# The same steps of a chunk-attention and two-layer kernel in another written order

## The chip, the cores and the metric

The kernel runs on one core of a Trainium2 chip. The metric is the device time of one execution in microseconds (us); lower is better. Before the change, three runs took 275.24, 275.53 and 278.67 us; their median is 275.53 us. The profile below is of one execution of its own.

## The reference

Attention inside chunks of 64 tokens, for 8 batches, 8 heads, 576 tokens and a head size of 64, and then two dense layers with a leaky ReLU between them on all 4608 tokens:

```python
q_c = q.reshape(B, H, nc, chunk, D)          # chunk = 64, nc = 9; k and v alike
scores = scale * np.matmul(q_c, k_c.transpose(0, 1, 2, 4, 3))
scores = scores - np.max(scores, axis=-1, keepdims=True)
attn = np.exp(scores)
attn = attn / (np.sum(attn, axis=-1, keepdims=True) + 1e-09)
out = np.matmul(attn, v_c)
x = out.transpose(0, 2, 1, 3).reshape(B * S, H * D)      # 4608 x 512
h = x @ w_in                                             # 512 x 2048
g = np.maximum(0.01 * h, h)
return g @ w_out                                         # 2048 x 512
```

Inputs and output are float32 in HBM.

## The kernel before, in words

**Groups.** The 4608 tokens are cut into 36 groups of 128 (two chunks each). Group `u` goes through a row of small stages, each a step of its own: loads of its q and k rows (`arrive`, 0 for q and 1 for k, issued on POOL, which also converts them to fp16; a group that crosses a batch has two DMAs for each), transposes of q and k, the scores (`s`, PE, eight small matmuls into `Sp`), their maximum and the subtraction (`m`, `b`, DVE), the exponential (`x`, ACT), sum and reciprocal (`z`, DVE), the normalisation (`n`, POOL or DVE, tile `en`), a transpose of the weights, the product with v (`v`, PE, into `xp`) and its copy into `xT` (`a`, ACT). For groups 0 to 9 q and k are transposed on PE (`pe_t`) and copied out (`p` into `QZ`, `k` into `KT`); from group 10 on SP issues transposing DMAs for both (`t`, into `QT` and `KT`) and POOL copies q on into `QZ` (`p`). The weights are transposed on PE for groups 0 to 7 and groups 8, 9 and 18 (`e`, copied by `d2`), else by a transposing DMA on SP (`d`, into `et`).

**Start.** q and k of group 0 come in float32 by DMAs of SP and ACT (L149) and are cast. The v rows of batch 0 are loaded in five pieces (`v_t`, L127) and placed chunk by chunk into the block-diagonal buffer `VB` (`v_p`, ACT, DVE or POOL); the other quarters of both `VB` buffers and of `QZ` are filled with zeros (`zv`, `zq`). v of a later batch comes in two DMAs (`v_in`, L111). `w_in` comes in four blocks of 512 columns, each in two halves (`Q`, L135), and `w_out` in four blocks of 512 rows (`P`, L141).

**Layers.** The tokens form 12 blocks: four of 128 and eight of 512. Blocks 0 to 3 are plain: 16 matmuls of 128 columns for each quarter of the first layer (`mm1`, L187, into `hT`), leaky ReLU on ACT (`g`, into `gT`), the second layer in quarters (`mm2`, L212, into `oP`). Block 4 and 5 have the plain first layer in pieces of 256 tokens. From block 6 on the first layer, and from block 4 on the second, use a seven-product scheme (Strassen's, in Winograd's form): sums of inputs (`xf`, tile `XF`, L285), of hidden values (`sf`, tiles `S` and `gT`) and of weights (`vf`, `wf`, tiles `VF` and `WF`), products (`f`, L325, into `hA`, `hB`, `hC`; `m2`, L373, into `oA`, `oB`, `oC`), and additions of the results on DVE and ACT. Stores go out from SP (`save`).

**The order of the work.** Every step is created once, by `add`, with an engine and a function that emits its instructions. Nothing is planned at run time: `ORDER` is a written list of 1403 entries, and `run` emits step after step from it:

```python
for i, fill, *slots in ORDER:
    s = steps[i]
    if fill:
        idle(fill[0], BANKS[fill[1]])
```

Each engine executes its own instructions in this order, and each instruction waits for what it needs. So the place of a step in the list sets what stands ahead of it on its engine; a step that waits holds up all behind it on that engine, DMA issues on POOL and SP included. The slots name the PSUM bank or the temporary tile. `fill` puts matmuls on constants ahead of a PE step (`idle`, L538; so many units of 128 columns); they are executed whether PE would have to wait or not. `ON` says which engine takes a step that can run on several.

## Time and profile before

| | us |
|---|---|
| median of three runs | 275.53 |
| profiled execution, its span | 275.67 |
| PE, busy | 263.9 |
| DVE, busy | 209.4 |
| ACT, busy | 196.3 |
| POOL, busy | 158.2 |

The page gives a span of 275.7 us and nothing around it. PE, DVE, ACT, POOL and SP are TensorE's matmuls, VectorE, ScalarE, GpSimd and SyncE; PEld is TensorE's weight load, which overlaps the matmuls. Engines run side by side, so their shares don't add up. L187 is line 187 of the kernel. In a timeline a row has start, duration, engine, line and operation, output and input, count and, in brackets, how long the engine idled before and what ended that. A DMA is issued by an engine and lands later; the time from issue to landing has its own view. The last matmul ends at 272.2 us; an eviction on ACT of 0.38 us and a store follow.

### The profile page before, as it was taken

The page shows a single profiled execution, that of the slowest core. Times are in us where ns is not written, and L with a number is a line of the kernel's source. Part 1 is how long each engine was busy: PE and PEld are TensorE (multiplying, and loading weights), DVE is VectorE, ACT ScalarE, POOL GpSimd, SP SyncE. Part 2 cuts the span into 40 slices and gives each one's busy share as a digit, 9 for nine tenths or more (in the row PEclk, how much of TensorE's full clock was granted, in tenths as well). Part 3 has the DMA queues.
Part 4 walks back from the last instruction along what each step waited for, and adds up shares of the span by engine and source line. Part 5 has one row for each costly group of instructions (what it writes and reads, how often), then busy time and mean ns, then how long its engine had stood idle before and what let it go on. Part 6 is the DMA issues. An engine that isn't in the chain of part 4 may idle for free.

```text
span 275.7 us, 7655 instructions
## 1 busy us (share of the span) xinstructions
PE 263.9 (96%) x3099; PEld 230.8 (84%) x3099; DVE 209.4 (76%) x376; ACT 196.3 (71%) x370; POOL 158.2 (57%) x199
## 2 busy tenths in 40 slices
PE   4899999999999999999799999999999999999994
PEld 2459678788898899999799999999999989888884
DVE  5786276878889898799778997889998873825462
ACT  6478964767844834899698558899787897467821
POOL 8989685595999991928927888626752020000000
PEclk9999999999999999999999999999999999999999
DMA  9999999999999999999999999969972051040016
GB/s 133 158 190 179 179 167 175 134 157 168 172 160 148 173 173 183 132 138 223 129 131 198 138 173 199 153 148 131 212 154 40 0 137 58 0 155 0 30 49 231
DMA packets 163635, 38.64 MB, mean 140 GB/s; under 512 B 154640, under 2 KB 159248, under 8 KB 163600
## 3 DMA queue, kind: packets, MB, share of 16 engines
q0 software_dynamic: 114384, 18.09, 101.9%
q1 hardware_dynamic: 48176, 19.80, 40.1%
q8 instruction: 24, 0.39, 0.6%
q10 hardware_dynamic: 1040, 0.26, 0.4%
q14 instruction: 11, 0.09, 0.1%
HBM read 36.70 MB, written 9.44 MB: 167 GB/s over the span
## 4 chain that ended last, share of the span: by engine, by line
PE 87%; DMA 5%; ACT 5%; POOL 1%; issue 1%; POOLq 0%
PE oA L373 20%; PE hA L325 14%; PE hT L187 13%; PE oC L373 10%; PE hC L325 7%; PE oB L373 5%; PE oP L212 5%; PE hB L325 4%; PE Sp L453 3%; DMA KT<-k_in 3%; PE xp L519 3%; DMA k_in<-in_k_dram 2%; PE idle L538 1%; ACT VB L118 1%; ACT xT L532 1%; ACT gT L198 1%
## 5 line engine op out<-in xcount | busy, mean ns | idle before, releaser
L373 PEld LDWEIGHTS <-gT 128*128 128x128 f16 x640 | 61.3, 98 | 6.7
L489 POOL TENSOR_TENSOR en<-ex,zi 128x512 f16<-128x512 f16 x23 | 26.5, 1153 | 48.4 <-DVE zi L483 17.3
L237 DVE TENSOR_TENSOR tmp<-hC,tmp 128x512 f32<-128x512 f32 x48 | 32.1, 683 | 20.0 <-PE hC L325 18.3
L187 PE MATMUL hT<-xT,w_inT 128*128 128x128 f16 (+1 forms) x512 | 46.0, 246 | 1.0 <-ACT xT L532 0.9
L187 PEld LDWEIGHTS <-w_inT 128*128 128x128 f16 x512 | 39.4, 98 | 4.7 <-issue 1.3
L325 PEld LDWEIGHTS <-VF 128*128 128x128 f16 x512 | 39.4, 98 | 2.7
L93 POOL DMA_DIRECT2D q_in<-in_q_dram x39 | 33.6, 866 | 5.2 <-DMA w_outT<-in_moe_w_out_dram 2.1
L93 POOL DMA_DIRECT2D k_in<-in_k_dram x39 | 33.6, 865 | 2.3 <-DMA k_in<-in_k_dram 1.2
L446 POOL COPY QZ<-QT 64x512 f16<-64x512 f16 x52 | 33.2, 639 | 2.7 <-DMA QT<-q_in 0.5
L201 ACT ACTIVATE tmp<-hA 128x512 f32<-128x512 f32 x48 | 27.7, 598 | 8.6 <-PE hA L325 8.0
L198 ACT ACTIVATE gT<-hT 128x512 f16<-128x512 f32 x48 | 26.7, 601 | 8.6 <-PE hT L187 8.6
L373 PE MATMUL oA<-WF,gT 128*128 128x256 f16 x256 | 32.5, 273 | 0.0
L325 PEld LDWEIGHTS <-w_inT 128*128 128x128 f16 x384 | 30.2, 98 | 2.3
L463 DVE TENSOR_REDUCE mx<-Sp 128x8 f32<-128x512 f32 x36 | 24.5, 682 | 8.6 <-PE Sp L453 8.5
L198 ACT ACTIVATE gT<-tmp 128x512 f16<-128x512 f32 x48 | 29.6, 629 | 1.2 <-DVE tmp L237 1.2
L473 ACT ACTIVATE ex<-sh 128x512 f16<-128x512 f32 x36 | 22.7, 629 | 10.3 <-DVE sh L467 10.1
L479 DVE TENSOR_REDUCE z<-ex 128x8 f32<-128x512 f16 x36 | 24.3, 676 | 6.2 <-ACT ex L473 6.1
L325 PE MATMUL hA<-XF,VF 128*128 128x128 f16 (+1 forms) x256 | 27.5, 246 | 0.0
L532 ACT ACTIVATE xT<-xp 128x512 f16<-128x512 f32 x36 | 21.2, 599 | 8.7 <-PE xp L519 8.6
L373 PEld LDWEIGHTS <-S 128*128 128x128 f16 x256 | 24.5, 98 | 2.7
L467 DVE TENSOR_TENSOR sh<-Sp,mx 128x512 f32<-128x512 f32 x36 | 24.4, 683 | 0.5
L201 ACT ACTIVATE hB<-hA 128x512 f32<-128x512 f32 x24 | 13.9, 586 | 12.2 <-PE hA L325 12.1
(77 smaller groups left out, 490.3 us busy)
## 6 DMA issues: line engine op xcount, KB each, us to landing
out_dram<-osb SPq DMA_DIRECT2D x14, 512.0 KB, 4.3
VB<-in_v_dram POOLq DMA_DIRECT2D x14, 288.0 KB, 7.8
q_in<-in_q_dram POOLq DMA_DIRECT2D x31, 128.0 KB, 7.4
k_in<-in_k_dram POOLq DMA_DIRECT2D x31, 128.0 KB, 7.2
w_inT<-in_moe_w_in_dram POOLq DMA_DIRECT2D x8, 256.0 KB, 7.6
w_outT<-in_moe_w_out_dram POOLq DMA_DIRECT2D x4, 512.0 KB, 9.4
out_dram<-osb SPq DMA_DIRECT2D x6, 256.0 KB, 4.9
v_t<-in_v_dram POOLq DMA_DIRECT2D x4, 128.0 KB, 7.6
```

The source lines that it names most:

```text
L93: nc.gpsimd.dma_start(out=t[a - u * G:z - u * G], in_=src[b, :, r:r + z - a, :].rearrange("h p d -> p h d"))
L187: nc.tensor.matmul(out=hT[:, i, :], lhsT=w_inT[:, t, fc * 128:(fc + 1) * 128], rhs=xT[:, t, r0 % RING:r0 % RING + tb], start=(i == 0 and t ...
L198: nc.scalar.activation(out=to, in_=of, func=AFT.Prelu, bias=0.0, scale=1.0, alpha=0.01)
L201: nc.scalar.activation(out=to, in_=of, func=AFT.Copy, bias=0.0, scale=1.0)
L237: (nc.vector if e == "dve" else nc.gpsimd).tensor_tensor(out=to, in0=a, in1=b, op=ALU.add)
L325: nc.tensor.matmul(out=PA[key][:, c, :], lhsT=w[:, t, fc * 128:(fc + 1) * 128], rhs=x[:, t, :], start=(m in (1, 5) and c == 0 and t == 0), ...
L373: nc.tensor.matmul(out=to, lhsT=lhs[:, fc, p * 128:(p + 1) * 128], rhs=rhs[:, fc, :], start=(fresh and fc == 0), stop=(fc == HB - 1), skip ...
L446: nc.gpsimd.tensor_copy(out=QZ[u % NQZ][part, :, :, s, :], in_=QT[u][part].rearrange("p i (e t) -> p i e t", e=2))
L463: nc.vector.tensor_reduce(out=MX[u], in_=SP[u], axis=AXL.X, op=ALU.max)
L467: nc.vector.tensor_tensor(out=SH[u], in0=SP.pop(u), in1=MX.pop(u).unsqueeze(2).to_broadcast((128, 8, CH)), op=ALU.subtract)
L479: nc.vector.tensor_reduce(out=z, in_=E[u], axis=AXL.X, op=ALU.add)
L489: eng.tensor_tensor(out=E[u], in0=ex, in1=ZI.pop(u).unsqueeze(2).to_broadcast((128, 8, CH)), op=ALU.mult)
```

## The change

The steps are the same 1403, with the same shapes. `ORDER` and `ON` are written anew, and the code around them is shortened.

**The order in the front.** By names (for `arrive`, q1 is group 1's q rows), POOL had:

```
q1 k1 k2 Q0 Q0 identity q2 q3 v0 v1 v2 k3 Q1 zq3 Q1 Q2 Q2 q5 v3 v_p v_p v_p q4 P0 zv k5 P1 zv zv zv
k4 q6 k7 v4 P2 k6 v_p q7 Q3 Q3 v_in1 v_in1 P3 q8 ...
```

and has now:

```
identity q3 q2 k1 k2 q1 k5 k3 v1 v0 v2 Q1 Q2 Q2 Q1 Q0 Q0 q4 v_p v_p v3 q5 v_p v_p k4 P0 n3 v_p Q3 Q3
v_p P1 P2 k7 q7 k6 v4 q6 v_in1 v_in1 P3 v_p n4 k8 ...
```

PE had, up to the first pieces of the layers (fillers in brackets, in units of 128 columns):

```
[21] k0 q0 q1 k1 [3] s0 k2 s1 [47] q3 q2 e0 [13] s2 [9] e1 [9] v0 k3 [6] v1 mm1(0,0) mm1(1,0) s3 mm1(0,1) e2
mm1(1,1) v2 mm1(0,2) mm1(1,2) mm1(2,0) q4 ...
```

and has now (`mm1(j,a)` is block j, quarter a of `w_in`):

```
[32] q0 [2] k0 [14] s0 q2 q3 [19] k1 [9] k2 [9] q1 [23] s2 [4] s1 k3 e0 k5 [25] s3 [44] v0 [6] e1 [13] v1
[2] mm1(0,1) e2 mm1(1,2) v2 mm1(0,2) mm1(2,1) mm1(0,0) mm1(2,0) q4 q5 e3 mm1(1,1) mm1(2,2) k4 v3 mm1(1,0)
mm1(3,1) mm2(0,0) mm1(3,2) s4 mm2(2,0) s5 mm1(3,3) ...
```

All fillers together were 108 units and are 202. ACT now has, from the first placed v row to the second xT: `v_p zv d2(0) k3 v_p v_p x1 v_p v_p v_p v_p x2 d2(1) a0 a1`, then `g a2 x3`.

**The order later.** DVE now has, around group 10: `m10 wf1 b10 n9 sf(4,0) d2(9) sf(4,1) z10 m11 b11 m12 z11 b12 m13 n11 b13`; it had `m10 b9 b10 z8 z9 vf0 z10 n10 sf(4,0) sf(4,1) sf(4,3) m11 b11`. PE has, around group 9: `v9 m2(4,5) s11 mm1(5,6)`; it had `v9` directly before block 5's `mm1`. SP had `save(4,1) t22q t23q d19 save(5,0) t22k d20` and has `t22q save(4,1) t22k t23q t24q d19 save(5,0) t23k d20`; near group 33 it had `t33q save(7,1) t33k t34k t34q d30 save(7,0)` and has `t33q t34q save(7,0) t35q t33k d30 t34k`.

**The engines.** 191 steps are on POOL instead of 186, 296 on DVE instead of 301; PE, ACT and SP keep their number. Seven of the 32 `xf` sums move from DVE to POOL: two of block 6, one of block 7, two of block 8, one each of blocks 10 and 11. As many `n` steps as before, 23, are on POOL, but others: `n3`, `n4` and `n7` come to it. Four `zv` fills and one `zq` fill leave POOL, and of the 18 `v_p` copies it has seven instead of four.

**The code.** Tiles that rotated through one tag with several buffers get a tag for each buffer, chosen by the group's or block's number; the windows of two q tiles become single tiles; branches that were never taken go (loads of pairs of q rows among them). Some steps name more of what they wait for, which matters to whoever plans an order and not to the instructions:

```diff
-    def k_tile():
-        return sbp.tile([128, H, D], FP16, name="k_in", tag="k_in", bufs=NIN)
+    def in_tile(what, u):
+        return sbp.tile([128, H, D], FP16, name=what, tag=f"{what}{u % NIN}", bufs=1)
...
+    IN_Q: dict[int, bass.AP] = {}
+    IN_K: dict[int, bass.AP] = {}
...
     def load_q(u):
-        load_rows(q_tile(u), q, u)
-        qk[u] = (q_tile(u), qk[u][1] if u in qk else None)
+        IN_Q[u] = in_tile("q_in", u)
+        load_rows(IN_Q[u], q, u)
...
-    def x_form(j, h, i):
+    def x_form(j, h, i, e):
...
         def less(to, a, b):
-            (nc.gpsimd if j >= POOL_X else nc.vector).tensor_tensor(out=to, in0=a, in1=b, op=ALU.subtract)
+            minus(to, a, b, e)
...
-        E[u] = sbp.tile([128, 8, CH], FP16, name="en", tag="en", bufs=3)
+        E[u] = sbp.tile([128, 8, CH], FP16, name="en", tag=f"en{u % 3}", bufs=1)
...
     ORDER = [
-        (55, 0), (0, 0), (56, 0), (62, 0), (1, 0), (59, 0), (60, 0), (64, 0), (61, 0), (2, 0), (57, 0), (63, 0), (65, 0), (3, 0), (66, 0), (4, 0), (52, 0), (5, 0),
...
+        (5, 0), (61, 0), (55, 0), (7, 0), (58, 0), (6, 0), (57, 0), (63, 0), (66, 0), (1, 0), (2, 0), (52, 0), (83, (32, 7), 0), (0, 0), (54, 0), (53, 0),
...
-        p1 = mm(1, 0, xs + gone(j) + [get(("fast", x)) for x in fast_n[-LIMIT:-LIMIT + 1]], [A], spare=SPARE + 1)
+        p1 = mm(1, 0, xs + gone(j) + w11 + [get(("fast", x)) for x in fast_n[-LIMIT:-LIMIT + 1]], [A], spare=SPARE + 1)
...
-                out_.append(add(key + (name, p), "act", us[0], emit, [of[p]] if last else of, key=7.0 + k0 / 100, take=T[name] if p == 0 else []))
+                out_.append(add(key + (name, p), "act", us[0], emit, [of[p]] + out_ if last else of, key=7.0 + k0 / 100, take=T[name] if p == 0 else []))
...
-                add(("xf", j, h, i), "pool" if j >= POOL_X else "dve", 1.6 if j >= POOL_X else dve, lambda j=j, h=h, i=i: x_form(j, h, i),
+                e, us = on(("xf", j, h, i), "dve", dve=0.40 if wide == 512 else 0.34, pool=1.6)
+                add(("xf", j, h, i), e, us, lambda j=j, h=h, i=i, e=e: x_form(j, h, i, e),
```

## The prediction

> **What bounds the kernel now.** I read the page first: the span, the busy shares and the slices.

> ```profile
> span 275.7 us, 7655 instructions
> PE 263.9 (96%) x3099; PEld 230.8 (84%) x3099; DVE 209.4 (76%) x376; ACT 196.3 (71%) x370; POOL 158.2 (57%) x199
> PE   4899999999999999999799999999999999999994
> DMA  9999999999999999999999999969972051040016
> ```

> PE is full in every slice but the first two, one near the middle and the last. DMA is full for 26 slices too, so transfers can still hold PE up. To see how much room is left I summed PE by stretches (after the stretch: its length, then the busy time of PE, PEld, DVE, ACT and POOL, the granted clock, DMA and GB/s) and listed what PE waited for after 20 us (total, times, longest).

> ```profile
> 0.00:20.00 20.00, 14.69 (x112) 8.29 (x113) 14.22 (x34) 12.06 (x23) 17.55 (x29) 1.00 1.51 160
> 20.00:272.20 252.20, 249.21 (x2993) 222.55 (x2989) 195.18 (x343) 183.91 (x347) 140.61 (x171) 1.00 1.44 139
> 272.20:275.70 3.50, 0.02 (x1) 0.00 (x0) 0.00 (x0) 0.38 (x1) 0.00 (x0) 1.00 0.38 135
> ```
> ```profile
> PE Sp L453 <- DMA KT<-k_in: 1.7, 1, 1.7
> PE hT L187 <- ACT xT L532: 0.9, 2, 0.7
> PE tpe L497 <- ACT gT L198: 0.3, 1, 0.3
> ```

> So the time is a sum of four terms: the start of the first layer's matmuls (20.0, below); PE's work from there (249.2); the waits in it (252.2 - 249.2 = 3.0, of which the three rows name 2.9); and 3.5 of last eviction and store. The granted clock is 1.00 in every stretch. Because every step is kept, with its shapes, the 249.2 can't be reordered away. The change can move only the start and the waits.

> The start, from the timelines of PE, POOL and ACT (start, duration):

> ```profile
> 1.46 2.42 PE L538 MATMUL idle<-XF 128*128 128x512 f16 x6 [1.46 <-DVE zeros L157]
> 5.94 0.58 PE L411 MATMUL kp<-ident,k_in 128*128 128x128 f16 x4 [2.06 <-POOL ident masks.py:199]
> 9.92 0.61 PE L411 MATMUL kp<-ident,k_in 128*128 128x128 f16 x4 [1.05 <-DMA k_in<-in_k_dram]
> 10.76 4.16 PE L538 MATMUL idle<-XF 128*128 128x512 f16 x12
> 18.75 0.39 PE L519 MATMUL xp<-et,VB 128*128 128x64 f16 x8
> 18.98 0.39 PE L411 MATMUL kp<-ident,k_in 128*128 128x128 f16 x4
> 19.98 2.17 PE L187 MATMUL hT<-xT,w_inT 128*128 128x128 f16 x32
> ```
> ```profile
> 1.24 1.07 POOL L93 DMA_DIRECT2D q_in<-in_q_dram  x1 [0.79 <-POOLq L1160]
> 5.26 0.27 POOL masks.py:197 MEMSET ident<- 128x128 f16 x1
> 5.60 0.29 POOL masks.py:199 TENSOR_SCALAR_AFFINE_SELECT ident<-ident 128x128 f16<-128x128 f16 x1
> 7.61 2.65 POOL L127 DMA_DIRECT2D v_t<-in_v_dram  x3
> 14.41 0.61 POOL L135 DMA_DIRECT2D w_inT<-in_moe_w_in_dram  x1 [0.15 <-issue]
> ```
> ```profile
> 16.84 2.44 ACT L118 ACTIVATE VB<-v_t 64x256 f16<-64x256 f16 x6
> 19.31 0.60 ACT L532 ACTIVATE xT<-xp 128x512 f16<-128x512 f32 x1
> 19.93 0.63 ACT L473 ACTIVATE ex<-sh 128x512 f16<-128x512 f32 x1
> ```

> The first hT starts when ACT has written xT of the first group (19.31 + 0.60 = 19.9). Ahead of that ACT places v rows for 2.4. The second stretch above begins there, at 20.0.

> Two pieces of the chain of waits (start, duration) give the price of a first-layer piece, 16 matmuls of 128 columns, and of a second-layer piece:

> ```profile
> 30.41 0.86 PE oP L212 x4
> 35.63 0.89 PE hT L187 x16
> ```

> **The front, step by step.** The identity now precedes all loads on POOL: 5.26 to 5.84 was 0.6, so the first load goes out at 1.8 instead of 1.2. Then come ten row loads (q3 q2 k1 k2 q1 k5 k3 v1 v0 v2) where before there were eight with two weight halves among them. The DMA view of short windows gives the issue-to-landing times (count, KB, us) of the first row load, of the third v load and of the last half of the third weight block:

> ```profile
> q_in<-in_q_dram POOLq DMA_DIRECT2D x1, 128.0 KB, 4.9
> ```
> ```profile
> v_t<-in_v_dram POOLq DMA_DIRECT2D x1, 128.0 KB, 7.5
> ```
> ```profile
> w_inT<-in_moe_w_in_dram POOLq DMA_DIRECT2D x1, 256.0 KB, 8.3
> ```

> POOL needs 0.88 per row load (2.65 / 3). Before, v2 was issued at 9.4 and landed at 16.9, and the last half of block 2 at 14.4 + 8.3 = 22.7. Between them lie one row and four halves, 5.8 in all; with 0.6 for the row a half takes 1.3. After, v2 is the tenth load: issued at 1.8 + 9 x 0.88 = 9.7, landing between 14.6 (4.9 later) and 17.2 (7.5 later). I take the middle, 15.9, because the queue is filling then. The first matmuls now want w_in block 1, whose second half is the fourth behind v2: 15.9 + 4 x 1.3 = 21.1. Block 0, which had lain ready early, lands last, at 15.9 + 7.8 = 23.7; its first user stands four matmul pieces later (21 + 4 x 0.89 + 0.5 = 25), so that is covered by 1.3.

> ACT gives nearly the same start. v1 lands two loads ahead of v2, at 14.2. Then ACT's written order to the first xT is seven v copies (2.44 / 6 = 0.41 each, 2.9), a zero fill, two copies and an exponential (2.4 by the 0.60 and 0.63 rows): 19.5. Then exponential, copy and xT, 1.8: 21.3. PE's own queue gives it a third time. It holds 202 filler units, against 108. The first 32 are slow (2.42 / 21 = 0.115 each): 1.46 + 3.7 = 5.1. The other 170 at 0.055 (0.89 / 16) are 9.4, with 1.0 on top while the clock is still low, and of 17 small stages four take 0.6 and thirteen 0.23 (18.75 to 18.98): 5.4. That is 20.9. So the start is **21.3**, between 20.0 (landing at 14.6) and 22.6 (17.2). Seventeen small PE stages instead of fifteen lie ahead of it, so PE's remaining work falls by 2 x 0.23: 248.75.

> [...]

> **The waits.** The longest, 1.7, is a K transpose that stood on SP behind an output store:

> ```profile
> 124.47 1.20 SPq L508 DMA_TRANSPOSE et<-en  x1
> 126.61 0.38 SPq L385 DMA_DIRECT2D out_dram<-osb  x1
> 127.16 1.96 SPq L433 DMA_TRANSPOSE KT<-k_in  x1
> ```

> This is group 22's; in the new order it stands before that store and before the et transpose at 124.47, so it goes out at least 2.7 earlier and the 1.7 goes. The other two follow v stages:

> ```profile
> 75.71 1.91 PE L187 MATMUL hT<-xT,w_inT 128*128 128x256 f16 x16 [0.69 <-ACT xT L532]
> 89.71 0.49 PE L187 MATMUL hT<-xT,w_inT 128*128 128x256 f16 x3 [0.22 <-ACT xT L532]
> ```

> The 0.69 was group 9, whose xT was wanted straight after its v stage; now a layer-2 piece and a score stage stand between (1.1), so it goes too. The 0.22 of group 11 stays: two score stages and the v stage itself, 0.7, lie ahead of the user in both orders.

> New ones are late next, at about 73 to 92 us. Counted in PE pieces, the score stage of group 10 moves 5 us back and its v stage only 2. DVE's queue between them is now: maximum, a weight difference, subtract, normalise of group 9, a layer-2 sum, a copy, another sum, and group 10's normaliser. Two groups of instructions (busy, mean ns of one, idle before) and a row of the DMA issues price these:

> ```profile
> L237 DVE TENSOR_TENSOR S<-gT 128x2048 f16<-128x2048 f16 x8 | 10.0, 1252 | 1.4 <-ACT gT L198 1.4
> L467 DVE TENSOR_TENSOR sh<-Sp,mx 128x512 f32<-128x512 f32 x36 | 24.4, 683 | 0.5
> L489 POOL TENSOR_TENSOR en<-ex,zi 128x512 f16<-128x512 f16 x23 | 26.5, 1153 | 48.4 <-DVE zi L483 17.3
> ```
> ```profile
> et<-en SPq DMA_TRANSPOSE x25, 5.1
> ```

> The pieces ahead put the score of group 10 at 69.1 and its v stage at 84.1. From 69.4, four steps of 0.7, three of 1.25 and 0.8 of small ones bring DVE to 76.8; POOL's normalise, 1.15, and the transpose, 5.1, to 83.1. One us is left for all hand-overs, and two K transposes stand close behind on SP. I allow 0.3 each for groups 9 and 10, 0.4 for group 11 (its et transpose is behind those two), 0.2 for its xT and 0.2 for a layer-2 sum that ends about one us before its use: **1.4**, between 0.2 (only group 11's xT) and 3.0 (as many as before).

> **Moves between engines.** Seven of the 32 input sums go from DVE to POOL. Their smallest form on DVE is this:

> ```profile
> L285 DVE TENSOR_TENSOR XF<-xT,XF 128x256 f16<-128x256 f16 x8 | 2.6, 328 | 0.0
> ```

> POOL running that form isn't in the trace: at least 0.33 by this row, at most about 2.3 by twice POOL's 1153 ns, which is the nearest row and whose 1.2 I take. Seven times that, 8, fits in the 48.4 that POOL idles before its normalise steps alone. Without that cover each load queued behind one would go out up to 2.3 later. In the front POOL loses five zero fills and gets three v copies more, which I count at nothing: it sits in the gaps between loads.

> Tile names with fixed slots instead of rotating ones reuse the same buffers in the same turn; I cost them at nothing, between -0.3 and +0.3, the size of one such wait.

> **Sum.** 21.3 + 248.75 + 1.4 + 3.5 = 274.95 of span. The median of before stands 0.15 below its profiled span (275.53 to 275.7), so **274.8**. With the bounds above, 20.0 to 22.6 and 0.2 to 3.0, it is 272.3 to 277.7.

> **Rivals.** Nothing ends late (chance 0.15): the start is halfway to the quickest landing, 20.6, and only group 11's wait is left: 20.6 + 248.75 + 0.2 + 3.5 - 0.15 = 272.9. For it: two of three named waits are removed by order alone. Against: three chains (weights, ACT, fillers) all end near 21.

> PE still slow (0.10): fillers are issued whether needed or not. If the clock comes up at 14 as before, the 37 units that fall between 8 and 14 cost 0.06 more each, 2.2, of which I let 0.4 hide behind loads: the start 23.1, the time 276.6. For it is the 0.61 at 9.92; against it, the gaps of 2.06 and 1.05 that kept PE from a steady run are filled now.

> POOL blocked, slower (0.17): the normalise step of group 3 now stands on POOL behind w_out block 0 and ahead of w_in block 3 and w_out blocks 1 and 2; before, DVE did it. That w_out block lands at 23.7 + 4 x 0.6 + 2 x 1.3 = 28.7, so it is issued 7.5 before, and POOL gets to the step at about 22.0. Its input waits for xT of group 2 (21.3, two pieces, two stages and 0.8: 24.4), the exponential and the normaliser, 0.6 + 1.2: 26.2; with 1.15 and a 0.4 copy the next load goes out at 27.8. That is 5.8 without an issue, against 2.6 of queue (7.5 - 4.9). The second half of block 3 then lands at 33.9 to 36.5, and is wanted at 21.3 + 13.6 = 34.9 (eleven pieces of 0.89, two of 0.86 and nine stages of 0.23). It decides from a landing after 34.9; every us later is paid once, and the w_out blocks behind it add theirs: 2 to 5, so 277 to 280, at the middle 278.3.

> Transposes late on SP (0.13): group 33's K transpose now stands behind a store and group 35's Q. If it or two others cost what the 1.7 did, 274.8 + 1.7 to 5.1: 276.5 to 280, middle 278.2.

> **Numbers.** The forecast keeps 0.45. From 272.6 to 279.5 all but the ends of the first rival and of the last two are held, about 2 in 10. A measurement of this kernel can tell about 2% from no change (270.0 and 281.0). Below 270.0 the start and the waits would have to lose 5.5 of 23.0 (20.0 + 3.0) while three chains end near 21: 0.02. Above 281.0: the tails of the last two rivals, 0.08. Within: 0.90.

> **What would show it.** The first hT at 21.3, released by ACT xT or by w_inT; PE busy 248 to 249 after it; no wait on KT at 133; small waits on xp or xT near 75 to 90; 3.5 after the last matmul. Wrong would be a wait on w_inT or w_outT near 35 to 40 (POOL blocked), fillers at over 0.1 a unit after 8 us (slow PE), or a wait of over 1.5 on KT or et.

## The result, and the profile after

The changed kernel takes 286.82 us (median; 283.35 to 289.61 over four executions) against 275.41 us for the kernel before. The ratio is 1.0339, with a 95% interval of 1.0247 to 1.0431: slower by 3.4%. The ratios leave out executions more than 1.5% above the fastest of their kernel, so they can stand below the quotient of two medians, and the profiles of four runs below (the K transposes first, the filled wait, all four repairs, the mended order with room) are of such longer executions, so that what they show holds for these executions.

The profiled execution took 286.58 us and has a span of 284.5. First the page: span, PE's share, and then the 40 slices of PE, of its granted clock and of DMA.

```profile
span 284.5 us, 7720 instructions
PE 270.0 (95%) x3124; PEld 231.9 (82%) x3124; DVE 210.4 (74%) x371; ACT 195.5 (69%) x370; POOL 162.8 (57%) x204
PE   7899998999996899999899899999999999999995
PEclk9999999999999799999999999999999999999999
DMA  9999999999999999999999999999792330101043
```

PE is nearly as full as before (95 and 96%), but not at the same places: there are dips in the 13th, the 20th and the 23rd slice, and the clock has a dip in the 14th (92 to 100 us). The sum by stretches, cut at the first hT and at the last matmul (length, busy time of PE, PEld, DVE, ACT, POOL, clock, DMA, GB/s):

```profile
0.00:21.26 21.26, 18.17 (x148) 9.52 (x149) 17.31 (x40) 16.88 (x31) 18.58 (x31) 1.00 1.53 154
21.26:281.01 259.75, 251.82 (x2976) 222.40 (x2976) 193.05 (x332) 178.28 (x339) 144.26 (x174) 0.99 1.34 134
281.01:284.50 3.49, 0.00 (x0) 0.00 (x0) 0.00 (x0) 0.38 (x1) 0.00 (x0) 1.00 0.36 130
```

So the start is 21.26, PE works 251.82, waits 259.75 - 251.82 = 7.93, and the tail is 3.49. The longest of these waits by what ended them (from 21.26 us on; total, times, longest):

```profile
PE xp L491 <- DMA et<-en: 6.0, 4, 2.8
PE hT L169 <- DVE sh L439: 0.5, 1, 0.5
PE qp L388 <- DMA q_in<-in_q_dram: 0.4, 1, 0.4
```

Six of the eight us are the values stage (`xp`) waiting for the transposed weights (`et`) of a group: 2.79 at group 11, 1.04 at 19, 1.98 at 21, 0.19 at 27. The wait for a K transpose that stood first before the change is gone. PE's timeline around the longest (start, duration; in brackets the idle time before), and the windows on both sides of 94.48:

```profile
93.04 0.41 PE L491 MATMUL xp<-et,VB 128*128 128x64 f16 x8 [2.79 <-DMA et<-en]
94.13 5.32 PE L169 MATMUL hT<-xT,w_inT 128*128 128x256 f16 x32 [0.22 <-ACT xT L504]
100.16 3.66 PE L169 MATMUL hT<-xT,w_inT 128*128 128x256 f16 x32
```
```profile
91.06:94.48 3.42, 1.22 (x28) 1.09 (x29) 3.35 (x5) 0.99 (x3) 2.81 (x4) 1.00 1.82 157
94.48:97.89 3.41, 3.41 (x19) 2.43 (x17) 3.38 (x6) 2.14 (x5) 3.41 (x4) 0.50 3.31 99
```

32 matmuls that take 3.66 us at 100 us took 5.32 at 94, since the clock was at half for 3.41 us. That is 3.41 / 2 = 1.7 us lost behind a wait of 2.79.

### The profile page after: what moved, and what is told of

It reads as the page before. It is cut to its first block, busy times and chain, and to the rows that moved or that the text cites. A ratio compares the mean times of both kernels' runs of the same rounds, so it can differ in the third digit from the quotient of the medians.

```text
span 284.5 us, 7720 instructions
## 1 busy us (share of the span) xinstructions
PE 270.0 (95%) x3124; PEld 231.9 (82%) x3124; DVE 210.4 (74%) x371; ACT 195.5 (69%) x370; POOL 162.8 (57%) x204
## 4 chain that ended last, share of the span: by engine, by line
PE 66%; DMA 13%; DVE 7%; ACT 7%; POOL 4%; issue 2%; POOLq 0%; DVEq 0%; ACTq 0%
PE oA L355 16%; PE hA L307 12%; PE hT L169 9%; PE oC L355 8%; DMA et<-en 8%; PE hC L307 6%; PE oB L355 4%; DMA q_in<-in_q_dram 4%; PE hB L307 3%; PE xp L491 3%; PE Sp L425 2%; DMA k_f<-in_k_dram 2%; POOL k_in L79 1%; PE oP L194 1%; DVE z L451 1%
## 5 line engine op out<-in xcount | busy, mean ns | idle before, releaser
L169 PE MATMUL hT<-xT,w_inT 128*128 128x128 f16 (+1 forms) x512 | 47.5, 250 | 0.8 <-DVE sh L439 0.5
L461 POOL TENSOR_TENSOR en<-ex,zi 128x512 f16<-128x512 f16 x23 | 24.7, 1073 | 32.5 <-DVE zi L455 14.6
L418 POOL COPY QZ<-QT 64x512 f16<-64x512 f16 x52 | 36.0, 696 | 5.6 <-DMA QT<-q_in 3.9
L451 DVE TENSOR_REDUCE z<-ex 128x8 f32<-128x512 f16 x36 | 24.4, 677 | 5.0 <-ACT ex L445 4.9
L445 ACT ACTIVATE ex<-sh 128x512 f16<-128x512 f32 x36 | 22.6, 631 | 6.0 <-DVE sh L439 5.8
L183 ACT ACTIVATE hB<-hA 128x512 f32<-128x512 f32 x24 | 13.7, 583 | 11.1 <-PE hA L307 10.4
## 6 DMA issues: line engine op xcount, KB each, us to landing
q_in<-in_q_dram POOLq DMA_DIRECT2D x31, 128.0 KB, 6.0
k_in<-in_k_dram POOLq DMA_DIRECT2D x31, 128.0 KB, 6.1
w_inT<-in_moe_w_in_dram POOLq DMA_DIRECT2D x8, 256.0 KB, 8.0
out_dram<-osb SPq DMA_DIRECT2D x6, 256.0 KB, 4.2
v_t<-in_v_dram POOLq DMA_DIRECT2D x4, 128.0 KB, 5.6
```

The source lines that it names most:

```text
L169: nc.tensor.matmul(out=hT[:, i, :], lhsT=w_inT[:, t, fc * 128:(fc + 1) * 128], rhs=xT[:, t, r0 % RING:r0 % RING + tb], start=(i == 0 and t ...
L183: nc.scalar.activation(out=to, in_=of, func=AFT.Copy, bias=0.0, scale=1.0)
L418: nc.gpsimd.tensor_copy(out=QZ[u % NQZ][part, :, :, s, :], in_=QT[u][part].rearrange("p i (e t) -> p i e t", e=2))
L451: nc.vector.tensor_reduce(out=z, in_=E[u], axis=AXL.X, op=ALU.add)
L461: eng.tensor_tensor(out=E[u], in0=ex, in1=ZI.pop(u).unsqueeze(2).to_broadcast((128, 8, CH)), op=ALU.mult)
```

## The experiments

**The old order in the new code.** The lists `ORDER` and `ON` of the kernel before, written into the changed kernel.

```diff
-    ON, ORDER of the change
+    ON, ORDER of the kernel before, by step name
```

> The changed kernel's code with the order and the engines of the kernel before written into it (54 steps go back to their old engine; tags and helper functions stay those of the changed kernel). Theory A (the loss lies in the written order alone): 275.4 us, within 0.3% of the kernel before, start at 20.0 us, no wait over 1.8 us. Rival (some of the loss comes with the code around the order, such as the fixed buffer tags): 277 us or more.

Measured: 275.69 us against 275.82, ratio 0.9995 (0.9969 to 1.0020). The profiled execution took 275.27 with a span of 273.5. By the same stretches:

```profile
0.00:19.04 19.04, 13.14 (x111) 7.56 (x112) 14.68 (x36) 12.49 (x23) 17.48 (x29) 1.00 1.55 158
19.04:270.06 251.02, 249.26 (x2994) 222.55 (x2990) 195.64 (x341) 183.61 (x347) 142.33 (x171) 1.00 1.41 140
270.06:273.50 3.44, 0.00 (x0) 0.00 (x0) 0.00 (x0) 0.38 (x1) 0.00 (x0) 0.86 0.37 134
```

The loss is in the two lists alone: within the interval, tags and shortened code cost nothing. Order and engines change together here and in the hybrids below, so what the engines of the 54 steps bear by themselves was not tested. This is also the better base: the execution profiled before the change started its first hT at 19.98 and waited 3.0, this one 19.04 and 1.76. Against it, the change costs 2.22 in the start, 6.17 in waits, 2.56 in PE's work and 0.05 in the tail: 11.0, the difference of the spans (284.5 - 273.5).

**The K transposes first.** SP's list around group 11:

```diff
-    t15q save(0,0) d10 t14k t15k d11 t16q
+    t15q save(0,0) t15k t14k d10 d11 t16q
```

> The changed kernel with SP's K transposes of groups 15 and 14 issued ahead of the et transpose of group 10 instead of behind it (two entries of the order move, nothing else). Theory A (group 11's et transpose is late because SP sat waiting for group 10's normalisation, and its two K transposes then went into the queue just ahead of it): it lands at about 90.3 us instead of 92.99, the wait of 2.79 us at group 11's values falls below 0.8, with it goes the 3.41 us of half clock, worth 1.7; up to 2 us of the gain may be given back at groups 21 and 23, whose et transposes wait for themselves: 282 to 284.5 us. Theory B (the transposes are slow because the two value loads of batch 3, issued at 80.81 and 82.55, share the transfer engines with them): it lands no earlier than 92, the wait stays over 2 us, 286 to 287.

Measured: 289.27 us, ratio 1.0377 (1.0289 to 1.0465). SP's timeline and PE's:

```profile
77.33 6.40 SPq L412 DMA_TRANSPOSE KT<-k_in  x2
83.82 2.67 SPq L480 DMA_TRANSPOSE et<-en  x2
```
```profile
90.78 0.61 PE L491 MATMUL xp<-et,VB 128*128 128x64 f16 x8 [4.72 <-DMA et<-en]
```

The rows for group 14's K transpose landed at 82.5 in this execution, SP stood at it until then, and now group 10's et transpose was late, by 4.72. Group 11's went out at 85.19 and landed at 92.51, which speaks against theory A and for theory B. But two transposes had still gone out just ahead of it, at 82.54 and 83.82, so this run doesn't separate the two; the next one does, since it leaves SP's list as it is.

**The value loads later.** POOL's list:

```diff
-    v_in3 p14 v_in3 k17 k16 p15 p15 q18
+    p14 k17 k16 p15 p15 q18 v_in3 v_in3
```

> The changed kernel with the two value loads of batch 3 issued on POOL behind the next three row loads, about 3 us later (needed first by group 13 at 109.5 us); SP's order stays. Theory B (the transposes are slow because these loads share the transfer engines): group 11's et transpose, issued at 84.9, takes about the median of 5.1 us instead of 8.10, lands near 90, the wait of 2.79 and the half clock behind it go: 282 to 284.5 us. Theory A (the place in SP's queue): it still takes 7 to 8 us, the wait stays over 2 us, 286 to 287.

Measured: 285.83 us, ratio 1.0353 (1.0314 to 1.0392). The DMA view in 0.1 us at the issue of group 11's et transpose, of the changed kernel and then of this one: the queue of POOL's loads and SP's queue (packets, MB, and the time that the packets took, added up, as a share of the time of 16 DMA engines, which can pass 100%), and the transpose's time to landing:

```profile
q0 software_dynamic: 100, 0.01, 199.5%
q1 hardware_dynamic: 5, 0.00, 9.7%
et<-en SPq DMA_TRANSPOSE x1, 8.1
```
```profile
q0 software_dynamic: 19, 0.00, 116.9%
q1 hardware_dynamic: 68, 0.02, 76.5%
et<-en SPq DMA_TRANSPOSE x1, 3.9
```

Theory B holds for this wait, and theory A falls: the K transposes of groups 14 and 15 still went out just ahead, at 81.35 and 82.64, and the transpose took 3.9 instead of 8.1. Over the whole flight of the transpose SP's queue has 56% in the changed kernel and 68% here, POOL's 149% and 106%: the two value loads held the engines while the transposes got less of them. Group 11 didn't wait, and the clock stayed full there. But the time didn't follow: 282 to 284.5 was expected. What was late next was a score bank that DVE frees, and group 21's transpose:

```profile
PE xp L491 <- DMA et<-en: 3.7, 2, 2.9
PE hT L169 <- DVE sh L439: 2.0, 1, 2.0
```

The 2.9 fell in group 21, and there the clock fell to half for 3.41 us.

**Filled wait.** Twelve idle products ahead of group 11's values (they took 2.75 us, from 90.73):

```diff
-    PE: m2(5,1) v11
+    PE: m2(5,1) [48 units] v11
```

> The changed kernel with 12 idle products (48 units of 128 columns, 2.56 us at full clock) ahead of group 11's values, so that TensorE works while it waits for the same transpose; nothing else. Theory C (the half clock of 94.5 to 97.9 us is set off by the idle 2.79 us, and costs about 1.7 us by itself): the clock stays full, the transpose lands at 93.0 as before, the span falls by 1.3 to 1.7 at 100 us, of which up to 1 may be given back at groups 19 and 21: 285 to 285.5 us. Rival (the clock falls for another reason, such as the power of the work behind it): the half clock stays, 286.5 to 287.

Measured: 287.05 us, ratio 1.0367 (1.0313 to 1.0422). The two windows here are the one behind group 11's wait and the one behind group 21's:

```profile
94.82:98.23 3.41, 3.19 (x34) 2.79 (x31) 3.38 (x5) 3.39 (x8) 3.41 (x4) 1.00 3.13 101
159.67:163.08 3.41, 3.41 (x35) 2.91 (x32) 0.06 (x1) 0.00 (x0) 3.32 (x6) 0.50 2.10 172
```

The clock stayed full at 94.8, so theory C holds: with the same work behind it and the idle time filled (0.62 us idle in the window ahead, 2.20 in the changed kernel's), the fall is gone. Group 11's values started 1.07 us later than in the changed kernel (94.11 against 93.04), group 16's scores 0.59 earlier (104.81 against 105.40): 1.66 won, as priced. It was given back at groups 19 and 21: group 21's values waited 3.21 and the clock fell there instead. My expectation of the total was wrong by that.

**Group 21 earlier.** Its normaliser, its normalisation and two transposes move; DVE and SP:

```diff
-    sf(6,1) xf(7) xf(7) xf(7) m22 xf(7) +u3 b22 +u3 sf(6,2) z21
+    sf(6,1) z21 xf(7) xf(7) xf(7) m22 xf(7) +u3 b22 +u3 sf(6,2)
-    d20 t25q t26q save(5,1) t24k d21
+    d20 d21 t25q t24k t26q save(5,1)
```

> The changed kernel with group 21's normaliser moved ahead of four input sums, three output sums, a maximum, a subtraction and a hidden-value sum on DVE (it ended at 148.3 us though its exponential was done at 139.9), its normalisation ahead of a value load on POOL, and on SP its et transpose and the K transpose of group 24 ahead of the Q transposes of groups 25 and 26. Theory A (the end of the run hangs on group 21's values, which come 1.98 us late, and this lateness is made by the written order of DVE, POOL and SP): the et transpose goes out near 142 instead of 151.74 and lands by 152, the wait of 1.98 goes; group 19's 1.04 and the 2.79 of group 11 stay: 283.5 to 285. Rival (the transfers are so full there that whatever is moved forward pushes another transfer late): a wait of 1.5 us or more comes at the next score stage or values stage, 286 to 287.

Measured: 284.82 us, ratio 1.0278 (1.0195 to 1.0361). The timelines of ACT, DVE and SP in the changed kernel show what was there: group 21's exponential, its sum eight us later, and two Q transposes of which the second stood until its rows had landed.

```profile
139.20 0.65 ACT L445 ACTIVATE ex<-sh 128x512 f16<-128x512 f32 x1
147.10 0.67 DVE L451 TENSOR_REDUCE z<-ex 128x8 f32<-128x512 f16 x1
142.01 7.35 SPq L409 DMA_TRANSPOSE QT<-q_in  x2
```

The 1.98 at group 21 went, a smaller wait, 0.85, came at group 23, and group 19's grew from 1.04 to 1.48; in sum PE waited 7.27 instead of 7.93. Theory A held for that one place.

**All four repairs.** That one, the later value loads, the maxima of groups 14 and 15 and the first one's subtraction (`m14 b14 m15`) ahead of a weight sum and a hidden-value sum on DVE, and

```diff
-    t23q t24q d19
+    d19 t23q t24q
```

> The changed kernel with four repairs of its order: the value loads of batch 3 three row loads later (as in the run of that alone), group 14's and 15's maximum and subtraction ahead of two weight and hidden-value sums on DVE (they held a score bank for 1.97 us once the first repair was in), group 19's et transpose ahead of two Q transposes on SP, and group 21's normaliser, normalisation and transposes early. Theory A (the loss behind the start is four or five waits, each made by one place in the order, and one fall of the clock): waits on et in sum below 2 us, the clock full from 6 us on, 277 to 280 us. Rival (the order is late as a whole by 70 us, and each repair uncovers the next wait): 282 to 285.

Measured: 284.13 us, ratio 1.0240 (1.0152 to 1.0328): the rival. PE's waits were still 8.07, at other places, and the clock fell once, behind group 23's wait:

```profile
PE xp L491 <- DMA et<-en: 2.3, 1, 2.3
PE Sp L425 <- POOL QZ L418: 2.3, 2, 1.4
PE oC L355 <- DVE osb L219: 1.5, 1, 1.5
```

**Where in the order.** Four hybrids, cut at an entry of `ORDER`; each step takes the engine that goes with its part.

```diff
-    ORDER = new
+    ORDER = new[:130] + the rest as in old       (and with 280)
+    ORDER = old[:280] + the rest as in new       (and with 130)
```

> The first 130 entries of the new order (to 27.5 us: the run of row loads and the run of weight blocks that the change is named after) with their engines, then all other steps in the old order with the old engines; 11 temporary buffers or banks are renumbered. Theory D (the front by itself costs only what it forecast, 1.3 us of later start less 0.5 of work done earlier, and the loss lies in the order behind it): 276 to 278 us, no wait over 2 us after 30 us. Theory E (the new front leaves rows and weights late, and that makes the waits at 90 to 160 us): 281 us or more.

> The first 280 entries of the new order (to 60.7 us), the rest in the old order; 12 buffers are renumbered. Theory D1 (the loss lies behind entry 280: DVE's, POOL's and SP's order around groups 10 to 21): 276 to 279 us. Theory D2 (by entry 280 the new order has fallen behind with the scores: group 10's stand at 70.75 us instead of 64.0, because its rows were loaded later): waits on et or QZ of 3 us or more in sum between 65 and 100 us, 280 us or more.

> The first 280 entries of the old order (to 59 us), then all other steps in the new order with the new engines; 9 buffers are renumbered. Theory G (the parts of the new order add their losses, and the part behind 60 us has its own: the new front with the old rest cost 6.3 us, so 4 to 5 are left): 279.5 to 282 us, with waits on et of 2 us or more in sum. Theory H (the later part is only late because the new front hands over late): 275 to 277.5 us, waits as in the kernel before.

> The first 130 entries of the old order (to 26 us), then the new order; nothing is renumbered. Theory G: the loss of the first 130 entries, 2.6 us, is gone and the rest stays, 283 to 285 us. Theory H: well below 281.

| kernel | us | ratio (95%) | first hT | PE's waits behind it | half clock |
|---|---|---|---|---|---|
| new to 130, then old | 278.91 | 1.0094 (1.0065 to 1.0122) | 21.87 | 2.64 | none |
| new to 280, then old | 282.57 | 1.0211 (1.0138 to 1.0284) | 21.76 | 4.86 | none |
| old to 280, then new | 285.96 | 1.0292 (1.0226 to 1.0357) | 18.80 | 8.91 | 2 x 3.41 |
| old to 130, then new | 287.26 | 1.0397 (1.0352 to 1.0441) | 18.29 | 9.52 | 1 x 3.41 |
| changed kernel | 286.82 | 1.0339 (1.0247 to 1.0431) | 21.26 | 7.93 | 1 x 3.41 |

The run of row loads and weight blocks costs 2.6 us by itself (1.0094 of 276.3), most of it a later start (21.87 against the control's 19.04): theory D in kind, 0.9 above its range. Theory E and theory H fall: the rest of the new order is slow behind the old front too. But theory G, by which the losses of the parts add, missed as well, by 4.0 and 2.3 us at the upper ends of its two ranges, and the new front to 280 fits neither of its theories: it took more than the 279 of the one, and its longest wait, 2.30, stays below the 3 of the other. The waits of the old front to 280 with the new rest show whose they are:

```profile
PE xp L491 <- DMA et<-en: 4.7, 4, 3.1
PE xp L491 <- DVE et L102: 1.4, 1, 1.4
PE xp L491 <- DVE osb L219: 1.0, 1, 1.0
```

The first and third rows are groups 10, 11, 19 and 21 again. The shares of the parts can't be read more closely than that, because a cut makes waits of its own: the 1.4 stands five us behind the cut, the hybrid with the new front to 280 waits 2.30 at group 7, at 67.5, and the one with the old front to 130 waits 2.05 and 1.30 for two K rows, at 28.8 and 31.9.

**Room instead of repairs.** Between a group's scores and its values on PE lie other pieces. At their own prices (0.87 for most, 0.44 for a product of the first layer, 0.23 for a small stage) they, with the scores themselves, are the room for the chain of DVE, ACT, POOL and SP. Group 11 had 14.3 us of room in the old order and has 12.3 in the new; group 21 had 27.9 and has 18.9. The chains took 15.9 and 22.5 in the changed kernel. Room alone doesn't decide: groups 32 and 33 have 14.0 and 13.6 in the new order and don't wait. One run gives room by moving only PE's stages (and with group 20's its copy on ACT):

```diff
-    m2(6,2) v20 v21 f(7) ... m2(6,4) v22
+    m2(6,2) f(7) ... m2(6,4) v20 v21 v22
```

> The changed kernel with the values stages of groups 20 and 21 moved on PE from behind the product m2(6,7) to just ahead of group 22's, some nine pieces (8 us) later; nothing else, no transfer and no sum moves. Their result is first needed by the input sums of block 8, after group 23's. Theory F (a wait is what PE's order leaves too little room for: without waits 18.9 us of PE work lie between group 21's scores and its values, the chain of DVE, ACT, POOL and the transposing DMA took 22.5): the wait of 1.98 us goes, the others stay, 284 to 285.5. Rival (the order is late as a whole, and what is won shows as the next wait, at group 23's or 24's): the sum of PE's waits stays at 8 us, 286 to 287.

Measured: 284.01 us, ratio 1.0291 (1.0202 to 1.0381). Group 21's wait is gone with nothing in its place; PE's waits are 5.80, and this holds for theory F. What is left on `et` is group 11's 2.96 and group 19's 1.19:

```profile
PE xp L491 <- DMA et<-en: 4.1, 2, 3.0
```

Two more begin the chains of groups 10 and 11 earlier (`p10` ahead of `n8` on POOL, `s10` and `s11` each six pieces of 0.87 earlier on PE, and what follows them), alone and together with all the rest:

> The changed kernel with the chain of groups 10 and 11 begun earlier: their four QZ copies on POOL ahead of or directly behind group 8's normalisation (where POOL idled 3.2 us), their scores on PE four and five pieces earlier, and behind them the maxima, subtractions, exponentials, normalisers, normalisations and et transposes. Theory F (the wait of 2.79 at group 11 and the fall of the clock behind it come from too little room between scores and values: 12.3 us of PE work against a chain of 15.9): the et transposes of groups 10 and 11 land 3 us or more ahead of their use, no wait on et before 130 us, the clock stays full at 93 to 100, PE's waits at 70 to 100 us fall from 5.7 us (clock included) to below 2: 282 to 284.5. Rival (the transfers hold it): group 11's et transpose still lands after 92.

> Both of these together with the repairs of the run before (value loads of batch 3 later, group 14's and 15's maximum and subtraction earlier, group 19's et transpose, group 21's normaliser earlier) and group 23's K transpose ahead of its Q transpose. Theory F (each wait is a chain with too little room, and room given at groups 10, 11, 20 and 21 removes waits without a new one): PE's waits after the start, 12.1 us with the clock in the changed kernel, fall to 4 to 6, and the time to 278 to 281. Rival (each repair uncovers the next wait): 10 us or more of waits are left, 283 to 285.

Measured: 285.54 us (1.0309, 1.0180 to 1.0437) and 285.29 us (1.0301, 1.0221 to 1.0381). In both of these runs groups 10 and 11 don't wait, and the clock stays full. But 7.40 and 6.60 us of waits are left, and both times missed theory F's ranges. In the second no wait for an et DMA stands among the long ones; these do:

```profile
PE hT L169 <- DVE sh L439: 1.8, 1, 1.8
PE oC L355 <- DVE osb L219: 1.5, 1, 1.5
PE hA L307 <- DVE XF L216: 1.3, 1, 1.3
PE xp L491 <- DVE et L102: 1.2, 1, 1.2
```

By the lists, each is made by a step that had been pushed back for one that was moved ahead. The last run mends these four:

> The order with room for groups 10, 11, 20 and 21, its own bad places mended: group 10's scores take a bank that is wanted 4 us later (PE had waited 1.8 us for it), group 9's et copy stands ahead of group 11's normaliser again (1.15), a sum of block 4's output ahead of two others (1.5), group 21's normaliser behind block 7's fourth input sum (1.3). Theory F (single waits, each with its place): these 5.7 us go, PE's waits after the start fall from 8.9 to 3 to 5 us, 279 to 281 us. Rival (each repair uncovers the next wait): 7 us or more are left, 283 or more.

Measured: 285.63 us, ratio 1.0316 (1.0247 to 1.0385). The four are gone, and others stand there:

```profile
PE Sp L425 <- POOL QZ L418: 3.7, 1, 3.7
PE oA L355 <- DVE S L216: 2.4, 2, 1.3
```

POOL had waited 5.74 us for group 24's Q transpose, and group 23's copies stood behind it. SP's list is that of the run before, where this transpose went out even later (136.34 against 135.63) and PE waited for nothing there: it took 3.73 us then and 7.52 here. Here a value load had gone out 0.20 us ahead of it, in the run before 0.39 behind it; whether that is the cause was not tested. The rival holds: repairs at single places moved the waits, and took 2.8 us off the median at the most, which the intervals don't separate from the changed kernel. No order with the new rest came below 284 us in the median, so why the new rest is late as a whole stays open.

## Why the prediction was wrong

The forecast was 274.8 us, the range 272.6 to 279.5. The profiled execution took 286.58, which is 11.8 more. By the sum's own terms: start 0.0 (21.26 for 21.3), PE's work +3.1 (251.82 for 248.75), waits +6.5 (7.93 for 1.4), tail 0.0, time against span +2.2 (2.08 above it for 0.15 below).

**The front: right, but against the wrong base.** The three estimates of the start, 21.1 by the weights, 21.3 by ACT and 20.9 by PE's fillers, met the run: the last half of `w_in` block 1 landed at 21.13, ACT's first xT ended at 21.12 and the last filler at 21.18. Which of the three set the 21.26 can't be told. The identity first, the ten row loads, the fillers and `n3` on POOL did what was worked out; PE waited neither on `w_outT` nor on `w_inT`. POOL blocked, the rival at 278.3, is out. So is PE still slow: the clock was full from 5.73 us on, against 13.73 in the profile before (the record of the clock begins with that rise, so the views print 1.00 ahead of it; eight idle products of 512 columns took 3.60 us there, at 1.46, and eleven took 2.54 behind it, at 16.10). In the twelve profiles with the new front it came up at 4.2 to 6.3 us, in the four with the old one, where PE waits 2 us and more among the first pieces, at 9.7 to 13.7. So the row at 9.92 told nothing of the new front: here it took 4.3 us, from the first filler at 1.46. The 1.0 us that the sum of the fillers sets on top for the low clock was an estimate that no run shows: in the changed kernel the first of those 170 units began at 5.80, behind the rise, and in its place PE stood idle for 1.6 us between the first filler and the first hT (21.26 less 18.17 busy, less the first 1.46). What the forecast took for the old start, 19.98, was a late one; the control has 19.04, so the front costs 2.2 and not 1.3.

**The waits: this step failed.** "New ones are late next, at about 73 to 92 us" was the right place and the right chain (group 10's and 11's scores later, values not, weight and hidden-value sums between). Its price was not: 1.4 us forecast, 7.93 measured. I took the median landing of an et transpose, 5.1, and got 0.3 to 0.4 a group. Group 11's took 8.1, because two value loads shared the engines (3.9 with these later). The median and the DMA slices, at 9 before as after, couldn't show that, for before the change group 11's had taken 5.54; the list could, since POOL's two loads of batch 3 went out at 73.49 and 83.90 and stand close together now, at 80.81 and 82.55. And I followed the chain for groups 9 to 11 only. Groups 19 and 21, whose transposes stood behind others on SP and of which the second had lost 9 us of room on PE, were never counted. The upper bound of 3.0, "as many as before", was the old order's sum and no bound for the new one.

**PE's work: this step failed too.** "The 249.2 can't be reordered away" overlooked that it can grow. A wait as long as 2.79 us brought the clock down for 3.41 us, 1.7 of the 3.1. Part of the other 1.4 goes with the number of waits: from the start of one piece to the start of the next, group 11's wait costs 2.95 over the price of the piece where its gap is 2.79, group 19's 1.21 for 1.04, group 21's 2.14 for 1.98. So each wait adds some 0.16 to what counts as PE's work. There are eleven over 0.1 us behind the start where the kernel before had four, which makes about 1.1, an estimate; the rest stays open. The runs whose clock stayed full agree: with the same matmuls, PE's work is 248.64 in the new front to 130, with four such waits, and 249.73 with groups 20 and 21 late, with eight.

**Time against span.** In every execution of which both are known the time stands 1.7 to 2.2 above the span (275.27 and 273.5 in the control). The median before and the span before were of different executions, and setting one against the other hid 2.2 us.

**The rivals.** Transposes late on SP (0.13) came nearest, with et transposes instead of K of 33 and Q of 35: it was the mechanism at groups 19 and 21, not at group 11, which went out 0.94 after its normalisation and was slow on the way. POOL's normalisations of groups 19 and 21, and their transposes on SP, which stood behind K and Q transposes and a store:

```profile
129.25 1.04 POOL L461 TENSOR_TENSOR en<-ex,zi 128x512 f16<-128x512 f16 x1 [1.79 <-ACT xT L504]
136.63 1.21 SPq L480 DMA_TRANSPOSE et<-en  x1
148.76 1.04 POOL L461 TENSOR_TENSOR en<-ex,zi 128x512 f16<-128x512 f16 x1 [3.21 <-ACT tmp L183]
151.74 1.21 SPq L480 DMA_TRANSPOSE et<-en  x1
```

That is 6.3 and 1.9 us on SP. The rival's 1.7 to 5.1 was 6.0 of waits with group 11's, and the clock came on top.

The removed waits went as forecast: no K transpose before the store is waited for, and group 9's 0.69 is gone. Group 11's wait for its xT, 0.22, stands in the timeline above to the digit. The input sums took POOL 0.67 us in the form of 256 columns and 1.15 in that of 512, where 1.2 was assumed.

## What to carry to other kernels

Read a written order as chains: for each group add up the work that the bounding engine has between the stage that starts a chain and the one that needs its end, and set it against the chain's length, with each transfer priced by what the list puts into flight beside it, not at its median (group 11's took 8.1 us here beside two value loads and 3.9 without them, at a median of 5.1 before). Do it for every group, since one order can be loose at ten places and tight at three. In this kernel a wait removed at one place mostly showed up at the next, so look at the sum of waits and the clock, not at the wait that was mended.

## What the runs showed of the hardware

```profile
91.11:94.52 3.41, 1.46 (x14) 1.06 (x11) 3.31 (x7) 0.10 (x1) 3.41 (x5) 1.00 2.52 168
94.52:97.93 3.41, 3.39 (x31) 3.05 (x32) 3.33 (x5) 3.35 (x7) 3.37 (x5) 1.00 2.96 118
```

So a gap's length alone didn't decide: 2.96 us at group 11 in the run with groups 20 and 21 late was cut by an edge into 1.53 and 1.43 (with 0.22 more behind it), and nothing fell:

```profile
88.24:91.65 3.41, 1.88 (x18) 1.43 (x15) 3.38 (x5) 0.00 (x0) 0.00 (x0) 1.00 1.92 148
91.65:95.07 3.42, 1.77 (x33) 1.59 (x34) 3.38 (x4) 1.55 (x4) 3.34 (x4) 1.00 1.97 159
95.07:98.48 3.41, 3.41 (x34) 3.06 (x32) 3.38 (x6) 2.83 (x7) 3.41 (x5) 1.00 3.16 102
```

2.79 us in the changed kernel lay with 2.20 in one window, and the clock fell. So in these profiles a window with 1.99 us idle and 1.42 busy was followed by half clock, and one with 1.95 idle and 1.46 busy was not.

The clock is part of why one kernel's executions differ, and not the whole: three of the changed kernel, with mean clocks of 1.000, 0.994 and 0.988, took 283.35, 286.58 and 287.06 us. The first two lie 3.2 apart, and a fall costs 1.7; of the run with the value loads later the longest, 286.87, has 1.000.
